# Strassen's scheme for the second products of the first layer's first pass, token sums in place, and a new table of the order

## The chip, the cores and the metric

The kernel runs on one core of one Trainium2 chip. The metric is the time of one execution on the device, in microseconds (us); of three runs of the kernel before, the median is 1659.44 us (1659.37 to 1663.88).

## The reference, cut to what matters

Attention within chunks of 64 tokens makes 4608 tokens of 512 features. Two feed-forward layers follow, the first with a gate.

```
scores = scale * q_c @ k_c.T ; attn = softmax(scores)        # per head and chunk of 64 tokens
x  = (attn @ v_c), heads side by side                        # 4608 x 512
g  = x @ w_gate ; val = x @ w_val                            # 512 -> 1536 each
x  = (g * sigmoid(g) * val) @ w_out                          # 1536 -> 512
h  = x @ w_in                                                # 512 -> 2048
out = (h * sigmoid(1.702 * h)) @ w_out2                      # 2048 -> 512
```

## The kernel before

Tokens are worked in nine blocks of 512, called block 0 to 8. Each layer's hidden features are worked in two passes over all blocks, so there are four passes: two of the first layer (three groups of two 128-feature tiles each), two of the second (two groups of four tiles). The first pass also does the attention, four units of 128 tokens for each block, one block ahead.

**Numbers in two parts.** Every operand of a large product is split into a high part of type fp32r and the rest (`split`: a copy, L573 on ACT, L575 on POOL, L577 on DVE, then a subtraction, L581). A product is three matmuls, high by high, high by rest and rest by high (`mm3`, L589, L590, L591).

**First products** (tokens by `w_gate`, `w_val`, or by `w_in`) go by Strassen's scheme in Winograd's form: seven products of sums of quarters in place of eight. `group_products` does them for a group, twelve matmuls of 256 columns to a product (token parts in tiles `x`, weight parts in `wa`, `wb`, `wc`). Of the seven, five go to one of the two PSUM banks on top of what is there; after the first, third and fifth, ACT copies the bank to a tile `u` (L573), and DVE adds four times a bank to a `u` (L581, `c<-u,banks`). The sixth product begins anew in the bank that the fifth has just filled, so it has to wait until ACT has copied the fifth.

**Second products of the first layer** come in two forms. In the first pass (`gated`, `second`) they are plain: the gated hidden tile is split, and each of the two tiles of a group is multiplied with four column blocks of `w_out`, three matmuls of 512 columns each, in four banks that add up over the three groups. In the second pass (`gated_quarters`, `hidden_part`, `second_part`) they go by Strassen's scheme: the hidden features of all three groups are collected in four quarters of 128 x 768, seven sums of quarters are split (128 x 768), and each gives three parts of six matmuls of 256 columns (21 parts for a block). The sums of `w_out` that they need are made beforehand (`y_combos`, `out_pair`), stored to `yw_dram` and loaded in pairs to the tiles `o` (L566). The first pass stores its sums to `y_dram`, the second adds to them.

**Order.** Every engine's queue is in a fixed order. A planner (`Program`) works out an order from costs and priorities, and then a table, `PLACES`, moves single operations behind others in an engine's queue, and some to another engine. So DVE or POOL may do what the code calls "dve" or "pool". SP issues all DMAs.

**Start and end.** While the first data come, TensorE does warm-up matmuls on an identity matrix (L1452, L1456). Attention units 0 to 3 are for block 0; unit 1 uses banks 4 and 5 (`gab`), where the first product goes as well. L863 are score blocks, L868 value blocks, L933 transposes, L916 to L924 the softmax. In the last block of the last pass, POOL and DVE add what the pass before left in `o_dram`, and the four quarters are stored.

Of the kernel before, what the change touches and what calls it, by code (L numbers as in the profile page):

```python
# [9 lines left out]
F32 = mybir.dt.float32  # L10
F32R = mybir.dt.float32r
# [12 lines left out]
def rd(ap):  # L24
# [34 lines left out]
    ),  # L59
    "dve": (  # L60
# [184 lines left out]
class Stage:  # L245
    UNIT = 256

    def __init__(self, pool, name, tags):
        self.ring, first = Ring(pool, name, 1), 0
        self.places = {}  # L250
        for tag, n in tags:
            self.places[tag] = Place(self, [first + 2 * i for i in range(n)])
            first += 2 * n
        self.size = first
# [14 lines left out]
class Place:  # L269
    def __init__(self, stage, homes):  # L270
        self.stage, self.homes, self.count = stage, homes, 0
# [1400 lines left out]
```

## Time and profile before

| | |
|---|---|
| median of three runs | 1659.44 us |
| profiled execution, its own time | 1666.5 us |
| its span, first to last instruction | 1664.6 us |
| PE busy | 1639.1 us, 98% of the span |
| DVE, ACT, POOL busy | 1218.1, 891.6, 527.3 us (73%, 54%, 32%) |
| moved by DMA | 488.98 MB, mean 294 GB/s |

The span is what the rows below add up to; the profiled execution's own time is 1.9 us more than it. Busy shares are means over stages with different loads, so a stage has to be read from its own stretch. An instruction's duration can reach into the next one's: matmuls of 0.28 us follow each other every 0.12 us.

### The profile page before, as it was taken

What the parts mean: (1) busy time and instruction counts of PE and PEld (TensorE: products, weight loads), DVE (VectorE), ACT (ScalarE), POOL (GpSimd) and SP (SyncE); (2) the same over time, 40 slices, a digit from 0 to 9 for tenths busy, and PEclk for the clock granted to TensorE, in tenths of its full rate; (3) what the DMA queues carried; (4) which work ended last, traced back from release to release, by engine and by line L of the source; (5) the groups of instructions that cost most, each with busy time, mean ns of one, the idle gap of its engine ahead of it and who ended that gap; (6) DMA issues with size and microseconds to landing.
All of it is one profiled execution on the core that took longest, in us unless ns stands there. A gap on an engine that the chain in (4) does not pass through costs nothing.

```text
span 1664.6 us, 37397 instructions
## 1 busy us (share of the span) xinstructions
PE 1639.1 (98%) x14914; PEld 1588.4 (95%) x14914; DVE 1218.1 (73%) x1895; ACT 891.6 (54%) x1514; POOL 527.3 (32%) x567
## 2 busy tenths in 40 slices
PE   8999999999999999999999999999999999999998
PEld 7889999999989999999999999999999999999998
DVE  7988788878745877777776877778755665566666
ACT  7977677677634444444433465555544444444443
POOL 1234554545531533332001104654521023211111
PEclk9999999999999999999999999999999999999999
DMA  7588888978799999999899999999878777767774
GB/s 298 172 286 315 300 276 300 322 266 289 264 355 336 306 357 354 364 331 356 302 326 378 359 344 316 319 319 313 286 228 334 275 250 232 230 212 235 242 267 135
DMA packets 191182, 488.98 MB, mean 294 GB/s; under 512 B 20000, under 2 KB 50208, under 8 KB 190752
## 3 DMA queue, kind: packets, MB, share of 16 engines
q1 hardware_dynamic: 191008, 486.59, 84.6%
q8 instruction: 118, 1.93, 0.5%
q14 instruction: 56, 0.46, 0.1%
HBM read 345.74 MB, written 140.77 MB: 292 GB/s over the span
## 4 chain that ended last, share of the span: by engine, by line
PE 82%; DMA 8%; DVE 5%; ACT 2%; issue 2%; POOL 1%; SPq 0%; POOLq 0%; DVEq 0%; ACTq 0%
PE banks L589 27%; PE banks L591 26%; PE banks L590 26%; DMA x_dram<-sp 2%; DMA o<-yw_dram 1%; PE banks L868 1%; PE banks L863 1%; DMA wd_b<-ws 1%; PE banks L933 1%; DMA x_dram<-xr 1%; DMA od_b<-ws 1%; ACT sp L573 1%; DMA o<-od_b 1%; DMA xr<-x_dram 1%; DMA xr<-y_dram 1%
## 5 line engine op out<-in xcount | busy, mean ns | idle before, releaser
L581 DVE TENSOR_TENSOR c<-u,banks 128x512 f32<-128x512 f32 x312 | 211.6, 682 | 169.7 <-PE banks L591 141.1
L589 PE MATMUL banks<-x,wc 128*128 128x256 f32 x1044 | 297.6, 285 | 1.9 <-ACT u L573 1.8
L590 PE MATMUL banks<-x,wc 128*128 128x256 f32 x1044 | 294.2, 282 | 0.1
L591 PE MATMUL banks<-x,wc 128*128 128x256 f32 x1044 | 294.1, 282 | 0.0
L573 ACT COPY u<-banks 128x512 f32<-128x512 f32 x261 | 151.5, 584 | 198.7 <-PE banks L591 198.3
L589 PE MATMUL banks<-x,wb 128*128 128x256 f32 x744 | 212.9, 286 | 5.0 <-ACT xr L573 2.0
L589 PE MATMUL banks<-x,wa 128*128 128x256 f32 x744 | 211.4, 284 | 0.3 <-DVE c L581 0.3
L590 PE MATMUL banks<-x,wb 128*128 128x256 f32 x744 | 210.7, 283 | 0.7 <-DVE x L581 0.7
L591 PE MATMUL banks<-x,wb 128*128 128x256 f32 x744 | 211.0, 284 | 0.0
L591 PE MATMUL banks<-x,wa 128*128 128x256 f32 x744 | 209.9, 282 | 0.0
L590 PE MATMUL banks<-x,wa 128*128 128x256 f32 x744 | 209.7, 282 | 0.0
L589 PEld LDWEIGHTS banks<-x,wc 128*128 128x128 f32 x1044 | 198.3, 190 | 7.5 <-ACT u L573 5.3
L590 PEld LDWEIGHTS banks<-x,wc 128*128 128x128 f32 x1044 | 198.5, 190 | 1.9 <-DVE x L581 0.3
L591 PEld LDWEIGHTS banks<-x,wc 128*128 128x128 f32 x1044 | 198.7, 190 | 0.0
L589 PE MATMUL banks<-sp,o 128*128 128x256 f32 (+1 forms) x594 | 195.1, 328 | 2.2 <-DMA o<-yw_dram 1.1
L590 PE MATMUL banks<-sp,o 128*128 128x256 f32 (+1 forms) x594 | 192.0, 323 | 1.2 <-DVE sp L581 1.2
L591 PE MATMUL banks<-sp,o 128*128 128x256 f32 (+1 forms) x594 | 192.0, 323 | 0.0
L1194 ACT ACTIVATE xr<-c 128x512 f32<-128x512 f32 x140 | 87.5, 631 | 156.7 <-DVE c L581 147.5
L589 PEld LDWEIGHTS banks<-x,wb 128*128 128x128 f32 x744 | 142.1, 191 | 8.5 <-DVE c L581 2.4
L590 PEld LDWEIGHTS banks<-x,wb 128*128 128x128 f32 x744 | 142.2, 191 | 2.3 <-DVE x L581 1.0
L589 PEld LDWEIGHTS banks<-x,wa 128*128 128x128 f32 x744 | 141.1, 190 | 2.8 <-DVE c L581 1.0
L591 PEld LDWEIGHTS banks<-x,wb 128*128 128x128 f32 x744 | 142.2, 191 | 0.0
(237 smaller groups left out, 4528.0 us busy)
## 6 DMA issues: line engine op xcount, KB each, us to landing
x<-x_dram SPq DMA_DIRECT2D x168, 512.0 KB, 5.8
o<-od_b SPq DMA_DIRECT2D x119, 512.0 KB, 4.6
o<-yw_dram SPq DMA_DIRECT2D x90, 512.0 KB, 5.6
x_dram<-x SPq DMA_DIRECT2D x63, 512.0 KB, 6.4
o<-od_a SPq DMA_DIRECT2D x48, 512.0 KB, 5.6
wd_b<-ws SPq DMA_DIRECT2D x56, 256.0 KB, 5.0
od_b<-ws SPq DMA_DIRECT2D x56, 256.0 KB, 4.9
x_dram<-sp SPq DMA_DIRECT2D x49, 256.0 KB, 5.5
```

The source lines that it names most:

```text
L573: op("act", act_us(n), lambda: nc.scalar.copy(out=dst.ap, in_=cut(src.ap)), [src], [dst], prio, near=near)
L581: lambda: {"dve": nc.vector, "pool": nc.gpsimd}[o.eng].tensor_tensor(out=dst.ap, in0=of_a(a.ap), in1=of_b(b.ap), op=by), reads or [a, b], ...
L589: nc.tensor.matmul(o, ah, bh, start=first, stop=False, **kind)
L590: nc.tensor.matmul(o, ah, bl, start=False, stop=False, **kind)
L591: nc.tensor.matmul(o, al, bh, start=False, stop=last, **kind)
L863: nc.tensor.matmul(un.s.ap[h64(b), a, h64(g)], un.q.ap[h64(a), cs], un.k.ap[h64(a), cs], start=True, stop=True)
L868: nc.tensor.matmul(un.o.ap[h64(b), a, h64(2 * g + c)], un.v.ap[h64(a), cs], un.e.ap[h64(a), cs], start=True, stop=True)
L933: nc.tensor.transpose(pt.ap[:, cs], e.ap[:, cs], ident.ap)
L1194: op("act", act_us(512), lambda: nc.scalar.activation(out=h.ap, in_=c.ap, func=AF.Gelu_apprx_sigmoid), [c], [h], prio, "gelu")
```

## The change

From block 3 on, the first pass also uses the scheme that the second pass has (`hides(p, b)`): its hidden features are kept as quarters, 21 parts of six matmuls of 256 columns take the place of 24 times three matmuls of 512 columns, the sums of its own `w_out` tiles are made and stored during the pass (`out_pair(0, g)`, `yw_dram[0]`), and loaded in eleven DMAs for a block in place of six. In `second_part` the seven results of the first pass are added up in tiles of `sf` and stored to `y_dram`.

Token sums (`x_made`) and sums of hidden quarters (`hidden_part`) are made in place, over a quarter that is no longer needed, so three tiles of token sums go and the token parts have seven tiles in place of eight. A sum in place may start only when the quarter it overwrites has been split. The order of the seven second products changes ("1326457"). At the start, unit 0 has banks 4 and 5 in place of unit 1, and eight more matmuls on the identity (`still`) stand among the first ones. Copies may be moved to any engine, as sums could before. The planner does 9 rounds in place of 12, and the table of moves is another one.

```diff
-        "4:9,44,61,22,19,21,8 5:26,10,18,24,17,27,52 7:13 11:15,6,20 78:54,69 23:28 25:16 209:244 "
+        "4:15,44,24,18 61:7,21,27 78:9,23,19,28 16:52 17:12,11,25,10,14,6,5,69 20:13,26 54:71 7038:244,209,210,86 "
...
-    ROUNDS = 12
+    ROUNDS = 9
...
-        ... ("o", 3), ("x", 8), ("c", 3), ("u", 3), ("m", 2), ("z", 2), ("xr", 1), ("xt", 3),
+        ... ("o", 3), ("c", 3), ("u", 3), ("m", 2), ("z", 2), ("xr", 1),
...
+    stage = {name: Stage(pool["sb"], name, tags) for name, tags in (
+        ("xs", (("x", 7, 4),)), ("sx", (("xt", 3),)), ("sh", (("h", 2), ("hx", 1))), ("sr", (("q", 1), ("k", 1), ("v", 1))),
+        ("sf", (("e", 2), ("yv", 2), ("x1", 1))), ("sp", (("hh", 3), ("hl", 3))))}
...
+    def hides(p, b):
+        return p == 1 or p == 0 and b >= 3
...
     def x_made(b, prio):
+        xb, made, q = xr.pop(b), {}, {}
+        for m in ORDER[1]:
+            made[m] = ring["x"].new([P, 2, 2, HT], F32R)
...
+        for m, j, n in (("1", 0, 0), ("2", 1, 0), ("3", 1, 1)):
+            parts(m, xb, quarter(j, n))
...
+        tt(t1, xb, xb, ALU.subtract, 512, prio, of_a=quarter(0, 1), of_b=quarter(0, 0), reads=[xb, made["1"]])
+        tt(t2, xb, t1, ALU.subtract, 512, prio, of_a=quarter(1, 1))
+        parts("6", t2)
+        parts("5", t1)
+        tt(t3, xb, xb, ALU.subtract, 512, prio, of_a=quarter(1, 1), of_b=quarter(0, 1), reads=[xb, t1])
+        parts("7", t3)
+        tt(t4, t2, xb, ALU.subtract, 512, prio, of_b=quarter(1, 0), reads=[t2, xb, made["2"]])
+        parts("4", t4)
...
-    YORDER = "1326574"
+    YORDER = "1326457"
...
     def hidden_part(y, label, prio):
+        src = {"1": b11, "3": b22, "2": b21, "6": b22, "4": b21, "5": b11, "7": b12}[label]
+        if label == "6":
+            tt(b22, b22, b11, ALU.subtract, 768, prio, T_ENG[1])
...
         elif label == "6":
-            tt(src, src, b21, ALU.subtract, 768, prio + 2, T_ENG[3])
+            tt(b21, b22, b21, ALU.subtract, 768, prio + 2, T_ENG[3])
...
+    def second_part(y, p, b, i, j, prio):
...
+        if p == 0:
...
+            if label in "1345":
+                t = ring["yv"].new([P, 2, HT])
+                if label == "5":
+                    tt(y.kept["3"], y.kept["3"], m, ALU.add, 512, prio + 0.5)
+                    done(y.kept["3"], 0, 1)
+                y.kept[label] = t
+                copy(t, m, 512, prio + 0.5)
+            elif label == "2":
+                tt(y.kept["1"], y.kept["1"], m, ALU.add, 512, prio + 0.5)
+                done(y.kept["1"], 0, 0)
+            elif label == "6":
+                tt(y.kept["3"], y.kept["3"], m, ALU.add, 512, prio + 0.5)
+            else:
+                tt(y.kept["4"], m, y.kept["4"], ALU.subtract, 512, prio + 0.5)
+                done(y.kept["4"], 1, 0)
+                tt(y.kept["5"], y.kept["5"], m, ALU.add, 512, prio + 0.5)
+                done(y.kept["5"], 1, 1)
+            return
...
-        attend(u, -40 + 4 * u, -60+3*u, bufs, ("sa", "gab", "yb", "ya")[u])
+        attend(u, -40 + 4 * u, -60+3*u, bufs, ("gab", "sa", "yb", "ya")[u])
+        if not u:
+            still = banks.new("ga", [P, 2, HT])
...
+            jobs = [(EARLY_PAIRS + STEP_PAIRS * j, out_pair(0, g)) for j, g in enumerate(gs)] + jobs
...
+    for i in range(8):
+        op("pe", 0.25, lambda: nc.tensor.matmul(still.ap[:, 0, :P], ident.ap, ident.ap, start=True, stop=True), [ident], [still], 9999)
```

Three places show what the table does. The first is PE's queue up to the first products, before and then now (`sf`, `c`: softmax tiles, `sr`, `sp`: q, k or v, `x`, later `xs`: the token parts, `wb`: weights).

```order
L933 MATMUL banks<-ident,c 128x128 x4
L1456 MATMUL banks<-ident 128x128 x5
L863 MATMUL banks<-sp 64x64 x16
L868 MATMUL banks<-c 64x64 x16
L589 MATMUL banks<-x,wb_285 128x256
```

```order
L978 MATMUL banks<-ident,c 128x128 x4
L1535 MATMUL banks<-ident 128x128 x4
L908 MATMUL banks<-sp 64x64 x16
L913 MATMUL banks<-sf,sr 64x64 x16
L913 MATMUL banks<-c 64x64 x16
L1707 MATMUL banks<-ident 128x128 x5
L908 MATMUL banks<-sr 64x64 x16
L628 MATMUL banks<-xs,wb_287 128x256
```

Both value blocks now stand together, and five of the new identity matmuls and a score block stand between them and the first product.

The second is PE's queue at the end of the last group of block 7 in the first pass, between the fifth product (`wc_1485`, now `wc_1427`) and the sixth (`wb_831`, now `wb_805`), before and then now.

```order
L590 MATMUL banks<-x,wc_1485 128x256
L591 MATMUL banks<-x,wc_1485 128x256
L589 MATMUL banks<-sp,o 128x512
L590 MATMUL banks<-sp,o 128x512
L591 MATMUL banks<-sp,o 128x512
...
L589 MATMUL banks<-x,wb_831 128x256
```

```order
L628 MATMUL banks<-xs,wc_1427 128x256
L629 MATMUL banks<-xs,wc_1427 128x256
L630 MATMUL banks<-xs,wc_1427 128x256
L628 MATMUL banks<-xs,wb_805 128x256
L629 MATMUL banks<-xs,wb_805 128x256
```

Before, two second products of three matmuls each stood there (the second, which reads the same, is left out); now the sixth product follows the fifth at once. In blocks 4, 5 and 6 four transposes stand there now, in block 3 a unit's value and score blocks, in block 8 a product of the next pass.

The third is DVE's queue in block 5, before and then now (`c<-u,banks`: sums of first products, `sr<-sr,c`, now `sx<-sx,c` and `sh<-sh,c`: gating, `sp`: rests of the hidden tiles, `t`, `st`, `ws`: weights).

```order
L924 TENSOR_TENSOR sf<-sf,z 128x512
L581 TENSOR_TENSOR c<-u,banks 128x512
L666 SCALAR_TENSOR_TENSOR t<-t,raw 128x256
L669 SCALAR_TENSOR_TENSOR t<-raw,t 128x256
L581 TENSOR_TENSOR c<-u,banks 128x512 x2
L581 TENSOR_TENSOR sr<-sr,c 128x512 x2
L581 TENSOR_TENSOR sp<-sr,sp 128x512
```

```order
L1430 TENSOR_TENSOR sx<-sx,c 128x2x256
L620 TENSOR_TENSOR c<-u,banks 128x512
L620 TENSOR_TENSOR xs<-xr,xs 128x512
L620 TENSOR_TENSOR sp<-sx,sp 128x768
L1430 TENSOR_TENSOR sh<-sh,c 128x2x256
L965 TENSOR_REDUCE z<-sf 128x8
L620 TENSOR_TENSOR sp<-sh,sp 128x768
L620 TENSOR_TENSOR sx<-sx 128x768
L620 TENSOR_TENSOR ws<-st,ws 128x256
L620 TENSOR_TENSOR sx<-sh,sx 128x768
```

Where there was a rest of 128 x 512 there are rests and sums of 128 x 768, and among them are rests of weights (`ws`) and of token parts (`xs`).

## Rows read from the trace of the kernel before

**Rows 1.** The page: engines, busy us and share.

```profile
PE 1639.1 (98%) x14914; PEld 1588.4 (95%) x14914; DVE 1218.1 (73%) x1895; ACT 891.6 (54%) x1514; POOL 527.3 (32%) x567
```

**Rows 2.** Waits of PE: engine, line, releaser, us in total, times, longest.

```profile
PE banks L589 <- ACT u L573: 2.5, 2, 1.8
PE banks L589 <- DVE c L581: 2.3, 3, 1.7
PE banks L589 <- ACT xr L573: 2.0, 1, 2.0
PE banks L589 <- DMA o<-yw_dram: 1.1, 3, 0.7
```

**Rows 3.** Windows: stretch, its us, busy us of PE, PEld, DVE, ACT, POOL, granted clock, DMA.

```profile
20.50:27.00 6.50, 6.49 (x57) 6.15 (x58) 5.88 (x13) 5.99 (x10) 2.39 (x2) 0.53 1.03 401
27.00:40.00 13.00, 11.12 (x171) 10.34 (x170) 11.82 (x22) 12.10 (x22) 1.49 (x2) 1.00 0.55 204
40.00:88.30 48.30, 48.20 (x512) 42.84 (x512) 46.77 (x77) 41.46 (x70) 15.22 (x11) 1.00 0.56 185
248.40:302.20 53.80, 53.80 (x597) 49.45 (x597) 44.80 (x71) 38.64 (x64) 29.09 (x36) 1.00 0.88 301
248.40:510.80 262.40, 260.24 (x2578) 238.57 (x2578) 193.80 (x312) 163.28 (x273) 121.89 (x143) 1.00 0.87 304
510.80:960.00 449.20, 444.56 (x3674) 440.17 (x3673) 344.52 (x505) 196.98 (x330) 111.11 (x119) 1.00 0.96 342
```

**Rows 4.** Timeline of PE: start us, us, instruction; plain and Strassen's second products.

```profile
324.12 0.39 PE L589 MATMUL banks<-sp,o 128*128 128x512 f32 x1
...
325.50 0.28 PE L589 MATMUL banks<-x,wc 128*128 128x256 f32 x1
...
622.00 0.28 PE L589 MATMUL banks<-sp,o 128*128 128x256 f32 x1
...
623.66 0.28 PE L591 MATMUL banks<-sp,o 128*128 128x256 f32 x1
```

**Rows 5.** Timeline around the first product.

```profile
19.87 0.59 ACT L573 COPY xr<-banks 128x512 f32<-128x512 f32 x1 [0.76 <-DVE x L581]
20.51 0.58 PE L589 MATMUL banks<-x,wb 128*128 128x256 f32 x1 [2.02 <-ACT xr L573]
21.10 0.41 PE L591 MATMUL banks<-x,wb 128*128 128x256 f32 x1
21.74 0.41 PE L591 MATMUL banks<-x,wb 128*128 128x256 f32 x1
```

**Rows 6.** Timeline in the second pass: a fifth and a sixth product with nothing between.

```profile
910.13 0.28 PE L591 MATMUL banks<-x,wc 128*128 128x256 f32 x1
910.50 0.59 ACT L573 COPY u<-banks 128x512 f32<-128x512 f32 x1 [5.17 <-PE banks L591]
911.14 0.39 PE L589 MATMUL banks<-x,wb 128*128 128x256 f32 x1 [0.73 <-ACT u L573]
```

**Rows 7.** Groups by form: busy us, mean ns of one, idle time before them.

```profile
L581 DVE TENSOR_TENSOR c<-u,banks 128x512 f32<-128x512 f32 x312 | 211.6, 682 | 169.7 <-PE banks L591 141.1 <-ACT u L573 24.6 <-ACT xr L1194 0.5
L581 DVE TENSOR_TENSOR sp<-sr,sp 128x768 fp32r<-128x768 f32 x34 | 32.8, 970 | 13.4 <-ACT sp L573 13.3
L581 DVE TENSOR_TENSOR ws<-st,ws 128x256 fp32r<-128x256 f32 x27 | 15.3, 571 | 3.5 <-POOL ws L575 3.5
L581 POOL TENSOR_TENSOR ws<-st,ws 128x256 fp32r<-128x256 f32 x73 | 62.6, 859 | 4.6
```

**Rows 8.** Timeline: POOL and DVE, both on SBUF, and DVE back to back.

```profile
11.58 0.68 DVE L666 SCALAR_TENSOR_TENSOR wc<-wc,wa 128x512 int32<-128x512 f32 x1
12.18 0.17 DVE L921 TENSOR_SCALAR z<-z 128x8 f32<-128x8 f32 x1
...
43.37 1.29 POOL L581 TENSOR_TENSOR ws<-wc,wc 128x512 f32<-128x512 f32 x1
43.52 1.70 DVE L669 SCALAR_TENSOR_TENSOR t<-wa,t 128x512 int32<-128x512 int32 x1
```

**Rows 9.** Timeline of the end.

```profile
1657.09 2.88 POOL L581 TENSOR_TENSOR t<-t,sf 128x512 f32<-128x512 f32 x2 [0.19 <-DVE sf L581]
1658.12 0.28 PE L591 MATMUL banks<-wb,xt 128*128 128x256 f32 x1
1661.00 0.44 SPq L569 DMA_DIRECT2D out<-t  x1
```

More of the change, by code (lines that the diff above doesn't have):

```diff
@@ L250, in __init__ @@
         self.places = {}
-        for tag, n in tags:
-            self.places[tag] = Place(self, [first + 2 * i for i in range(n)])
-            first += 2 * n
+        for tag, n, *size in tags:
+            size = size[0] if size else 2
+            self.places[tag] = Place(self, [first + size * i for i in range(n)], size)
+            first += size * n
         self.size = first
@@ L269, with __init__ @@
 class Place:
-    def __init__(self, stage, homes):
-        self.stage, self.homes, self.count = stage, homes, 0
+    def __init__(self, stage, homes, size):
+        self.stage, self.homes, self.size, self.count = stage, homes, size, 0
     def new(self, shape, dtype=F32):
-        b = self.stage.take(self.homes[self.count % len(self.homes)], 2)
+        b = self.stage.take(self.homes[self.count % len(self.homes)], self.size)
         self.count += 1
+        flat = b.make
         if len(shape) == 3:
-            flat = b.make
             b.make = lambda: flat().rearrange("p (a b) -> p a b", a=shape[1])
+        elif len(shape) == 4:
+            b.make = lambda: flat().rearrange("p (a b c) -> p a b c", a=shape[1], b=shape[2])
         return b
@@ L631, in attention_two_moe_kernel @@
             start[p].append(t)
-            t += sum(step_us(g, p) for g in gs) + (6.0 if p == 0 and b < NB - 1 else 0) + (3 * GV if p == b == 0 else 0)
+            t += sum(step_us(g, p, b) for g in gs) + (6.0 if p == 0 and b < NB - 1 else 0) + (3 * GV if p == b == 0 else 0)
     start.append([t])
@@ L722, in y_combos @@
         yield "3", s4, lambda ap: ap
-    yw_dram = pool["dram"].tile([P, 22, 2, 256], F32, name="yw_dram")
-    yw_done = [Buf(None) for _ in range(21)]
+    yw_dram = [pool["dram"].tile([P, 22, 2, 256], F32, name="yw_dram%d" % p) for p in range(2)]
+    yw_done = [[Buf(None) for _ in range(21)] for p in range(2)]
     W, WD, OD, WO = {}, {}, {}, {}
@@ L998, in token_combos @@
         b = [[quarter(j, n) for n in range(2)] for j in range(2)]
-        t1, t2, t4 = [ring["xt"].new([P, 2, HT]) for _ in range(3)]
+        t1, t2, t4 = [ring[t].new([P, 2, HT]) for t in places]
         tt(t1, xb, xb, ALU.subtract, 512, prio, of_a=b[0][1], of_b=b[0][0])
@@ L1012, in x_made, with quarter, parts @@
     def x_made(b, prio):
-        X[0, b] = []
-        for i, (m, src, cut) in enumerate(token_combos(xr.pop(b), prio)):
-            assert m == ORDER[1][i]
-            x = ring["x"].new([P, 2, 2, HT], F32R)
-            X[0, b].append(x)
-            split(*[x.part(lambda ap, c=c: ap[:, c]) for c in range(2)], src, 512, prio + i, "pool" if b else ("dve", "pool")[i % 2], cut)
-            store(x_dram[0][:, b, i], Buf(lambda x=x: x.ap.rearrange("p c a t -> p (c a t)"), None, None, x), [xd[0][b][i]], prio + i + 2)
+        xb, made, q = xr.pop(b), {}, {}
+        for m in ORDER[1]:
+            made[m] = ring["x"].new([P, 2, 2, HT], F32R)
+        X[0, b] = [made[m] for m in ORDER[1]]
+        def quarter(j, n):
+            return lambda ap: ap[:, 2 * j:2 * j + 2, n * HT:(n + 1) * HT]
+        def parts(m, src, cut=lambda ap: ap):
+            i = ORDER[1].index(m)
+            split(*[made[m].part(lambda ap, c=c: ap[:, c]) for c in range(2)], src, 512, prio + i, "pool", cut)
+            store(x_dram[0][:, b, i], Buf(lambda x=made[m]: x.ap.rearrange("p c a t -> p (c a t)"), None, None, made[m]),
+                  [xd[0][b][i]], prio + i + 2)
+        for m, j, n in (("1", 0, 0), ("2", 1, 0), ("3", 1, 1)):
+            parts(m, xb, quarter(j, n))
+        t1, t3, t4 = [Buf(lambda cut=quarter(j, n): cut(xb.ap), None, None, xb) for j, n in ((0, 0), (0, 1), (1, 0))]
+        t2 = ring["x1"].new([P, 2, HT])
+        tt(t1, xb, xb, ALU.subtract, 512, prio, of_a=quarter(0, 1), of_b=quarter(0, 0), reads=[xb, made["1"]])
[6 more added lines that the diff above has]
+        parts("4", t4)
     x0_dram = pool["dram"].tile([P, KD * BT], F32, name="x0_dram")
@@ L1058, in x_to_dram @@
             if b < NB - 1:
-                t = stage[2].take(n % 4 * 3, 2)
+                t = stage["sp"].take(n % 4 * 3, 2)
                 hi = Buf(lambda t=t: t.ap.rearrange("p (a t) -> p a t", a=2), t.prev, t.before, t)
@@ L1351, in hidden @@
         y = Hidden()
-        y.homes = [[stage[1].take(3 * n, 3) for n in range(2)], [stage[0].take(3 * n, 3) for n in range(2)]]
+        y.homes = [[stage[t].take(3 * n, 3) for n in range(2)] for t in ("sx", "sh")]
         return y
@@ L1358, in gated_quarters @@
             qs = [q.part(lambda ap: ap[:, js]) for q in y.homes[i]]
-            whole = stage[1 - i].now
+            whole = stage[("sx", "sh")[i]].now
             def ap(whole=whole):
@@ L1432, in second_part, with done @@
             return
+        label = YORDER[i]
+        if p == 0:
+            def done(t, r, c):
+                yd.setdefault(b, []).append(Buf(None))
+                store(y_dram[:, 2 * r:2 * r + 2, b * BT + c * HT:b * BT + c * HT + HT], t, [yd[b][-1]], prio + 1)
+            if label in "1345":
[16 more added lines that the diff above has]
+            return
         def add(r, c, by=ALU.add):
@@ L1436, in add @@
             tt(d, d, m, by, 512, prio + 0.5)
-        for args in (((0, 0),), ((0, 1),), ((0, 0),), ((0, 1),), ((1, 1), (0, 1)), ((1, 1), (1, 0)), ((1, 0, ALU.subtract),))[i]:
+        for args in {"1": ((0, 0),), "3": ((0, 1),), "2": ((0, 0),), "6": ((0, 1),), "4": ((1, 0, ALU.subtract),),
+                     "5": ((1, 1), (0, 1)), "7": ((1, 1), (1, 0))}[label]:
             add(*args)
@@ L1501, in spread @@
         jobs = [j for g in passes[p + 1][1] for j in group_to_dram(g, 0)]
-        a = start[p][0] + (100 if p == 0 else 10)
+        a = start[p][0] + (AFTER_PAIRS if p == 0 else 10)
         if p == 2:
@@ L1531, in put @@
                     if after_first and i == 0:
-                        for area, kind in zip(stage, (F32R, F32, F32R)):
-                            area.turn(kind)
+                        for area in ("sr", "sx", "sh"):
+                            stage[area].turn(F32R)
                 def at(i, tj=tj, step=step):
@@ L1545, in attention_two_moe_kernel @@
                         c = group_products(g, xs, at, put, p)
-                    if j == p == 0:
+                    if j == 0 and not hides(p, b):
                         yab = [banks.new("y" + i, [P, 2, BT]) for i in "ab"]
                         ys = [yab[e // 2].part(lambda ap, e=e: ap[:, e % 2]) for e in range(KD)]
-                    if p == 1:
+                    if hides(p, b):
                         if j == 0:
-                            if b == 0:
-                                for area, kind in zip(stage, (F32, F32, F32R)):
-                                    area.turn(kind)
                             hid = hidden()
```

80 lines of the change are left out of this document (32 added, 48 removed), and 360 rows, old and new, of the table PLACES.

## The prediction

> **What bounds the kernel now.** I read the page's line of engines first. PE is busy in 98% of the span; DVE comes next with 73% [rows 1]. Such shares are means, so the windows come next: in the stage that the change touches, 248.4 to 510.8 us (blocks 4 to 8 of the first pass), PE is busy for 260.24 of 262.40 us, DVE for 193.80, ACT for 163.28, POOL for 121.89 [rows 3]. PE is thus the bound there, and its time is the number of matmuls times their pitch. The list of waits agrees: the largest waits of PE are single ones, 2.5 us on the copy `u`, 2.3 on `c`, 2.0 on a bank of the attention, 1.1 on `yw_dram` loads [rows 2]. So two things can move the time: fewer columns for PE, and whether the others can still feed PE when they have more to do.
>
> **The change part by part, for the profiled execution.**
>
> *Fewer columns.* The pitch is read from starts, since durations overlap. Between 324.12 and 325.50 stand six plain matmuls of 512 columns: 1.38 / 6 = 0.230 us. Between 622.00 and 623.66 stand fourteen of 256 columns: 1.66 / 14 = 0.119 us [rows 4]. For one group of one block the plain form takes 24 x 0.230 = 5.52 us. Strassen's takes 21 x 6 / 3 = 42 matmuls for a group, 42 x 0.119 = 5.00. That saves 0.52 us, for 18 groups (blocks 3 to 8, three each) **9.4 us**. With a reading error of 0.01 us at either end of the first stretch the saving is 8.6 to 10.3.
>
> The Trainium skill (TensorE: Matmul & The Clock Gate, section Wait — 56ns, not 53.3ns?) puts the warm distance between starts at columns over 2.4 GHz plus 2.5 ns; by that a group would save 24 x 0.2158 - 42 x 0.1092 = 0.594 us, 18 groups 10.7 us, and the forecast would lie 1.3 us lower. The trace shows longer pitches, 0.230 and 0.119, and these decide.
>
> *The start.* The first product started at 20.51 us after a wait of 2.02 for unit 1's bank [rows 5]. The granted clock is 0.53 of full speed up to 27 us and 1.00 after it, which is the 1.2 GHz level and then 2.4; ahead of the first product PE had stood idle for those 2.02 us. From 21.10 to 21.74 three matmuls of 256 columns take 0.64 us, 0.213 each instead of 0.119 [rows 4, 5]. In 20.5 to 27 there are 57 matmuls in 6.49 us, and in 27 to 40 PE is idle for 1.9 of 13.00 us [rows 3]. Now unit 0 has the banks of the first product, both value blocks stand ahead, and then five identity matmuls and a score block: PE has work where it waited. I estimate the first product at 21.0 (five more small matmuls, 0.5 us). Some 24 matmuls of the first products fall before 27 us; at full clock they save 24 x 0.094 = 2.3 us, and the 1.9 us idle go in part, as the first weights no longer wait behind unit 1. Against that, four softmax operations of units 2 and 3 stand on DVE ahead of the token parts, up to 4 x 0.68 = 2.7 us [rows 8]. Bounds: -4.5 (all of 2.3 + 1.9, and 0.3 from score blocks at the higher clock) to +2.7; I take **-3**, nearer the gain, because the wait has work in its place.
>
> *The sixth product's gap.* It begins anew in the fifth's bank and waits until ACT has copied this. The second pass of before shows it uncovered: 910.13 to 911.14 is 1.01 us instead of 0.119, 0.89 lost [rows 6]. In blocks 1 to 7 second products used to stand there. Now nothing does at the last group of block 7 (0.89); four transposes do in blocks 4, 5 and 6, which I put at four matmuls of 256 columns at most (0.48), leaving about 0.45 each; score and value blocks or a product cover blocks 3 and 8. That is **+2.2**; if all covers fail, five such gaps, +4.4, and 0.9 with only block 7's.
>
> *DVE's load.* In blocks 4 to 8 DVE gets 50 more operations of 128 x 768 (0.970 us), 26 more `c`-like ones with a PSUM operand (0.682), 29 more rests of 256 columns (0.571) [rows 7], and 17 fewer of 512 in SBUF (0.68) [rows 8]: 48.5 + 17.7 + 16.6 - 11.6 = +71. POOL loses 64 by the same count, its `ws` rests at 0.859 among them [rows 7]. So DVE would need 193.8 + 71 = 265 us in 262.4 - 5 x 1.56 = 254.6 us. That is over 100%, but durations overlap: two DVE operations start 0.60 apart where the first is listed with 0.68 [rows 8]. With 0.08 less for each of 400 instructions the need is 233, **91% of the time**. Before it was 74%. That 97% can be had without PE waiting shows between 40 and 88.3 us: DVE busy 46.77 of 48.30, PE 48.20 [rows 3] (there overlaps count once); it is the nearest row. I put **+2** for late `c`, `sx` and token parts; bounds 0 (as in that row) and +32 (below, among the rivals).
>
> An operation of DVE on two SBUF operands beside one of POOL was listed with 1.70 us, where one alone has 0.68 [rows 8]. The Trainium skill (SBUF — State Buffer, section Who interferes with whom) says of this pair that a DVE instruction with two SBUF inputs contends with a POOL instruction that reads SBUF, and that one waits for the other as a whole. POOL has 64 us less in these blocks, so by row and rule alike part of the growth of DVE's busy time is given back; I count none of it in the need.
>
> *Token parts.* Seven tiles in place of eight: the parts of the next block are made over quarters that are just split, so a sum in place waits at the head of its engine's queue until ACT's copy and the rest of that quarter are done. Behind it on DVE stand the `c` sums, for whose banks PE waits. A late one shows as a wait of PE on `xs`. It is in the +2.
>
> *Transfers.* Eleven loads in place of six for each of six blocks, about 23 MB more of 489. The share of DMA in this stage, 0.87, would rise towards the 0.96 and 342 GB/s of the second pass [rows 3], where PE waited 1.1 us in all for `yw_dram` [rows 2]. I take the same again, **+1** (0 to 3). What SP now issues in addition stands in its queue ahead of later weight loads; those of before show no wait of PE beyond [rows 2].
>
> *Old waits.* The table is another, so the waits of PE between 248.4 and 960 us, 2.16 us idle in the first pass's blocks and 4.64 in the second pass [rows 3], can go or come. I take **-3**, a little under the half; bounds -7 (all of it goes) and +3 (half as much comes).
>
> *The end.* POOL takes two adds of 1.44 us before the last output, which is issued 1661.00 - 1658.12 = 2.88 us after PE's last matmul [rows 9]. In the new order POOL has three adds in series after the last label's sums, and these start 12 matmuls (1.4 us) before PE ends: 3 x 1.44 - 1.4 + some 0.9 of issuing and waiting gives 3.8. **+1** (0.3 to 1.5).
>
> Passes three and four keep their matmuls; I count nothing there.
>
> **Sum:** -9.4 - 3 + 2.2 + 2 + 1 - 3 + 1 = -9.2. The profiled execution's own time, 1666.5, lies 7.1 us above the median of the runs, 1659.44; I take that offset as the same for both kernels. 1666.5 - 9.2 = 1657.3 in the profile, and **1650 us** for the median.
>
> **Rivals.**
>
> *DVE becomes the bound (slower).* Place: blocks 4 to 8, where the most rests and sums are made in hidden quarters, each a link in a chain ACT copy, DVE rest, PE. For it: in block 4 of before (248.4 to 302.2) DVE's share was 44.80 of 53.80, 83%, with gaps that no instruction filled, since an in-order queue waits at its head. If the stage cannot be filled beyond 84%, it lasts 233 / 0.84 = 277 us, 23 over the 254.6, and the kernel 1650 + 23 - 2 = 1671. It decides from where 233 / share eats the saving of the other terms: 233 / (254.6 + 9) = 88%. Against it: the 97% between 40 and 88.3 us, and POOL, which is nearly free to DVE now. With the 265 of listed durations it would be worse, 1682 at 100%, but the starts speak against that count.
>
> *The gain comes back as waits (same).* The columns go, but loads of `yw_dram` and token parts made just in time each stop PE once per block: at 0.7 us, the longest wait on such a load [rows 2], 9 blocks give 6 us in place of 1, and the old waits stay: 1650 + 5 + 3 - 2 = 1656. For it: three `o` tiles only, and the DMA share of 0.96. Against it: in pass two the same loads cost 1.1 us in all.
>
> *More than forecast.* The start takes all of its 4.5 us and the old waits go to -7, no new ones on DVE: 1650 - 1.5 - 4 - 2 = 1642. For it: these waits are few and single, as a better table would remove them. Against it: every move is now made under tighter tiles.
>
> *The change does less than it says:* the column count is fixed by the program, so I give this no chance of its own.
>
> **How the numbers follow.** My forecast (1645 to 1654) has 0.49, more than forecast 0.18, gain given back 0.19, DVE as the bound 0.14. What a measurement can tell from no change is 0.3%, 5 us: faster is below 1654.4. So faster 0.67, same 0.19, slower 0.14. The range takes in the two near cases whole and the low end of the slow one's approach: 1640 to 1661.
>
> **What would show it.** In the profile after: 1.56 us less PE time in each of blocks 3 to 8, and a group's second products at 5.0 us; granted clock near 1.00 and no wait of 2 us at the first product; 0.9 us between a fifth and a sixth product at the end of block 7 and half of that in blocks 4 to 6; DVE at 85 to 95% of blocks 4 to 8 and PE still at 98%; waits on `yw_dram` of 1 to 3 us; last output issued 3.8 us after the last matmul. I am wrong if PE's idle time in blocks 4 to 8 is above some 8 us with DVE `c`, `sx` or `sp` as releaser, if the first stretch stays at the 1.2 GHz level, or if the pitch of the new second products isn't 0.119.

## The result, and the profile after

The changed kernel takes 1677.92 us (median of four runs, 1674.44 to 1680.13) against 1660.13 for the kernel before beside it: ratio 1.0102, 95% interval 1.0087 to 1.0117. It is 17 us slower where 9 us less had been forecast, and lies outside the range. The profiled execution took 1678.61 us, its span is 1676.8, so 12.2 us more than the span of before, which is what the rows below add up to. The medians differ by 17.8: the profiled execution of before lies 7.1 us above its median, that of after 0.7. The rows can't tell where the other 5.6 us stand.

The page's line of engines:

```profile
PE 1639.5 (98%) x15254; PEld 1604.5 (96%) x15254; DVE 1292.6 (77%) x2061; ACT 902.6 (54%) x1574; POOL 517.7 (31%) x505
```

DVE has 74 us more than in [rows 1]. PE's share still reads 98%, although it waits longer: a matmul's modelled duration reaches over short gaps. So lengths of stages are compared. The first pass's last second products stand among the first products of the second pass's first block (24 plain ones before, 126 of Strassen's after), so a border that both kernels reach with the same work done is the start of the second pass's second block. The windows of after are: from the first product to there (called the first pass below), from there to the third block of the third pass (called the second pass), from there to the last matmul, and blocks 4 to 8 (columns as in [rows 3]):

```profile
23.80:546.40 522.60, 511.41 (x5754) 487.10 (x5751) 453.29 (x794) 355.33 (x608) 149.34 (x157) 1.00 0.88 308
546.40:1014.60 468.20, 455.29 (x3723) 447.64 (x3723) 389.31 (x605) 212.15 (x381) 112.42 (x109) 1.00 0.99 359
1014.60:1670.00 655.40, 654.06 (x5480) 652.74 (x5478) 432.38 (x631) 320.40 (x564) 247.33 (x226) 1.00 0.79 266
238.20:500.30 262.10, 254.71 (x2848) 248.07 (x2847) 228.17 (x399) 171.09 (x296) 59.59 (x58) 1.00 0.93 325
```

The same windows of before, by the same borders:

```profile
20.50:546.50 526.00, 520.55 (x5453) 478.36 (x5454) 412.41 (x682) 355.19 (x593) 223.75 (x250) 0.99 0.84 289
546.50:1000.20 453.70, 448.28 (x3721) 444.24 (x3721) 353.54 (x520) 203.91 (x343) 106.38 (x111) 1.00 0.96 344
1000.20:1658.10 657.90, 655.27 (x5479) 652.08 (x5478) 438.02 (x669) 320.35 (x560) 191.75 (x196) 1.00 0.79 263
```

The first of these stages ends at about 546.4 us in both: what the columns saved was given back inside it. The second, whose matmuls did not change (3723 and 3721), became **14.5 us longer**; there DMA went from 0.96 to 0.99 and from 344 to 359 GB/s, DVE from 353.54 to 389.31 us. The rest is 2.5 us shorter; over all runs below this stretch takes 652.0 to 660.5 us, so a difference of this size means nothing. The end is 0.3 longer.

PE's waits after, to be read against [rows 2]:

```profile
PE banks L628 <- ACT u L616: 8.6, 11, 2.5
PE banks L628 <- DMA o<-yw_dram: 4.4, 10, 1.3
PE banks L629 <- DVE sp L620: 4.0, 8, 1.4
PE banks L1707 <- DVE xs L620: 2.4, 1, 2.4
PE banks L628 <- DVE c L620: 2.2, 4, 0.9
```

Instead of single waits there are many, on ACT, on DVE and on transfers. One of them in the second pass shows how they hang together, ACT's timeline first, then PE's:

```profile
844.98 0.84 ACT L616 CAST sp<-sh 128x768 fp32r<-128x768 f32 x1 [0.24 <-issue]
852.01 0.40 ACT L616 CAST ws<-st 128x256 fp32r<-128x256 f32 x1 [6.19 <-DMA od_b<-ws]
852.32 0.58 ACT L616 COPY u<-banks 128x512 f32<-128x512 f32 x1
```

```profile
850.77 0.28 PE L630 MATMUL banks<-sp,o 128*128 128x256 f32 x1
852.95 0.39 PE L628 MATMUL banks<-xs,wc 128*128 128x256 f32 x1 [1.90 <-ACT u L616]
```

A weight's copy (`ws`) waits 6.19 us at the head of ACT's queue, because the store that frees its tile has not landed; behind it stands `u`, and behind `u` PE. The wait is put down to ACT, and its cause is a transfer.

What the second pass moves more is mostly preparation of the third pass's weights. The DMA table of that stage, after and then before (x is the number of transfers, then KB each and us to landing):

```profile
DMA packets 68691, 168.07 MB, mean 359 GB/s; under 512 B 6883, under 2 KB 20481, under 8 KB 68644
wd_b<-ws SPq DMA_DIRECT2D x32, 256.0 KB, 5.3
od_b<-ws SPq DMA_DIRECT2D x28, 256.0 KB, 5.6
raw<-in_moe_w_in SPq DMA_DIRECT2D x22, 255.8 KB, 5.0
raw<-in_moe_w_out SPq DMA_DIRECT2D x16, 255.8 KB, 5.4
```

```profile
DMA packets 62122, 156.03 MB, mean 344 GB/s; under 512 B 6215, under 2 KB 16980, under 8 KB 62079
od_b<-ws SPq DMA_DIRECT2D x24, 256.0 KB, 5.4
wd_b<-ws SPq DMA_DIRECT2D x17, 256.0 KB, 5.7
raw<-in_moe_w_in SPq DMA_DIRECT2D x13, 255.8 KB, 5.1
raw<-in_moe_w_out SPq DMA_DIRECT2D x8, 255.8 KB, 6.3
```

That is 98 transfers in place of 62, 36 x 0.256 = 9.2 of the 12.0 MB more. In the first stage the changed kernel has none of the 27 `wd_b`, `od_b` and `raw<-in_moe_w_in` transfers that stood there before; it makes and loads its own `w_out` sums instead.

### The profile page after: what moved, and what is told of

It is laid out like the page before. It is cut to its first block, busy times and chain, and to the rows that moved or that the text cites. A ratio compares the mean times of both kernels' runs of the same rounds, so it can differ in the third digit from the quotient of the medians.

```text
span 1676.8 us, 38536 instructions
## 1 busy us (share of the span) xinstructions
PE 1639.5 (98%) x15254; PEld 1604.5 (96%) x15254; DVE 1292.6 (77%) x2061; ACT 902.6 (54%) x1574; POOL 517.7 (31%) x505
## 5 line engine op out<-in xcount | busy, mean ns | idle before, releaser
L628 PE MATMUL banks<-xs,wc 128*128 128x256 f32 x1044 | 298.5, 286 | 3.9 <-ACT u L616 3.2
L630 PE MATMUL banks<-xs,wc 128*128 128x256 f32 x1044 | 295.2, 283 | 0.0
L629 PE MATMUL banks<-xs,wc 128*128 128x256 f32 x1044 | 295.1, 283 | 0.0
L628 PE MATMUL banks<-xs,wb 128*128 128x256 f32 x744 | 212.1, 285 | 6.9 <-ACT u L616 5.4
L628 PE MATMUL banks<-sp,o 128*128 128x256 f32 (+1 forms) x702 | 210.6, 300 | 5.2 <-DMA o<-yw_dram 4.4
L628 PE MATMUL banks<-xs,wa 128*128 128x256 f32 x744 | 211.6, 284 | 1.1 <-DVE c L620 1.1
L629 PE MATMUL banks<-sp,o 128*128 128x256 f32 (+1 forms) x702 | 207.4, 295 | 4.1 <-DVE sp L620 4.0
L630 PE MATMUL banks<-xs,wa 128*128 128x256 f32 x744 | 210.0, 282 | 0.0
L630 PE MATMUL banks<-xs,wb 128*128 128x256 f32 x744 | 209.8, 282 | 0.0
L629 PE MATMUL banks<-xs,wb 128*128 128x256 f32 x744 | 209.7, 282 | 0.0
L629 PE MATMUL banks<-xs,wa 128*128 128x256 f32 x744 | 209.4, 282 | 0.0
L616 ACT COPY u<-banks 128x512 f32<-128x512 f32 x226 | 131.7, 584 | 142.9 <-PE banks L630 141.8
L628 PEld LDWEIGHTS banks<-xs,wc 128*128 128x128 f32 x1044 | 198.8, 190 | 8.7 <-ACT u L616 6.7
L630 PE MATMUL banks<-sp,o 128*128 128x256 f32 (+1 forms) x702 | 206.0, 293 | 0.0
L629 PEld LDWEIGHTS banks<-xs,wc 128*128 128x128 f32 x1044 | 199.5, 191 | 0.3
L630 PEld LDWEIGHTS banks<-xs,wc 128*128 128x128 f32 x1044 | 199.5, 191 | 0.0
L628 PEld LDWEIGHTS banks<-xs,wb 128*128 128x128 f32 x744 | 141.2, 190 | 9.8 <-ACT u L616 6.7
L628 PEld LDWEIGHTS banks<-xs,wa 128*128 128x128 f32 x744 | 141.4, 190 | 3.0 <-DVE c L620 1.9
L628 PEld LDWEIGHTS banks<-sp,o 128*128 128x128 f32 x702 | 133.0, 189 | 10.6 <-DMA o<-yw_dram 6.0
L629 PEld LDWEIGHTS banks<-xs,wa 128*128 128x128 f32 x744 | 141.3, 190 | 0.5
```

What stands on the lines that cost most here:

```text
L616: o = op(eng, us, lambda: on[o.eng](dst.ap, cut(src.ap)), [src], [dst], prio, near=near)
L628: nc.tensor.matmul(o, ah, bh, start=first, stop=False, **kind)
L629: nc.tensor.matmul(o, ah, bl, start=False, stop=False, **kind)
L630: nc.tensor.matmul(o, al, bh, start=False, stop=last, **kind)
```

## The experiments

Two theories are tried. LOAD says that the change adds work and bytes to engines that are already full (the expectations also call it FORM, ENGINE for ACT and DVE, DMA for the transfers). ORDER (also TABLE) says that the new form is worth its columns and the new order is bad. Ratios are to the kernel before, run beside each; lengths of a stage come from one profiled execution of each kernel, and stages that an edit leaves alone differ between such executions by 1 to 3 us in the first two and by up to 6 in the long last one. Cuts in code are marked `...`.

**Without tables.** `PLACES = {}` in e1 (before), e2 and e3 (changed); e3 also:

```diff
-        return p == 1 or p == 0 and b >= 3
+        return p == 1
...
-            jobs = [(EARLY_PAIRS + STEP_PAIRS * j, out_pair(0, g)) for j, g in enumerate(gs)] + jobs
+            jobs = jobs
```

> The kernel before without its table of moves (the planner's own order). It is the base for the next two. Theory FORM (the changed form and the sums in place make work for DVE, ACT and DMA that eats the columns saved, whatever the order): about 1690 to 1720 us, no statement on its distance to the changed kernel without table except that the changed one is not faster. Theory TABLE (the form is worth its 9 us, the new table is worse than the old one by some 20): the changed kernel without table is 5 to 10 us faster than this one.

> The changed kernel without its table of moves. TABLE: 5 to 10 us below the kernel before without table. FORM: at or above it, by 0 to 20 us.

> The changed kernel without table, and with plain second products in all blocks of the first pass (no sums of w_out for it, no eleven loads); sums in place, seven token tiles, the start and the planner's rounds stay as changed. Against the changed kernel without table it tells what the form alone is worth. If the form is worth its columns: 5 to 9 us slower than the changed kernel without table. FORM: equal or faster by up to 10 us.

Measured: 1700.44 (1.0244), 1724.22 (1.0388, interval 1.0364 to 1.0412) and 1711.34 us (1.0307, 1.0273 to 1.0340). With the planner's own order the form costs 12.9 us (FORM had said up to 10), and the rest of the change 10.9. TABLE falls: without tables the loss is larger, 23.8 us, and the new table is worth more to its kernel (46.3 us) than the old one to its own (40.3). From block 3 to the end of the first stage e2 takes 366.1 us and e3 354.8, so in this order most of the form's cost stands in the first pass.

**One tile less.** e11 is e1 with `("x", 7)` for `("x", 8)`.

> The kernel before without its table, with seven token tiles in place of eight and nothing else changed: against e1 (1700.4 us) the price of the missing tile. e3 stood 10.9 us above e1 with the plain form, of which some 12 us lay in blocks 3 to 18 (4.8 in the first pass, 6.8 in the second). If the missing tile is most of it: 1706 to 1712. If it is the sums in place or the weights' copies: 1698 to 1703.

1696.89 us (1.0211): not slower than e1, and a little below both forecasts. The missing tile alone is not the reason. What makes e3 slower than e1 stays open: the sums in place, the new start and the planner's rounds were not taken apart, and each changes the planner's order too.

**The preparation left out.** e14 is e2 without `out_pair(0, g)`; the loads read `od_a` tiles.

> The changed kernel without table as in e2 (1724.2 us), but without preparing the first pass's own sums of w_out: the eleven loads for a block stay, and take tiles of w_out that are there anyway (not the reference's values). Away are 42 copies and rests of weights, 12 sums of weights, 48 conversions, 21 stores and 12 loads, between 70 and 300 us. If this preparation is what the form costs (12.9 us between e3 and e2): 1704 to 1712, so the form alone would be worth nothing or a few us. If it is the eleven loads, the hidden sums and their place in the queues: 1718 to 1725.

1727.2 us (1.0408): a miss. The second pass moves 161.8 MB instead of 171.0 and still takes no less time (483.2 us, e2 475.8). In the planner's order a changed list of operations moves everything else, and differences of some us between e1, e2, e3, e11 and e14 can come from that alone; what the preparation costs stays open.

**Bytes taken away.** In the changed kernel's order:

```diff
-            load(x.part(lambda ap: ap.rearrange("p c a t -> p (c a t)")), x_dram[layer - 1][:, b, i], prio + 2 * i, [xd[layer - 1][b][i]])
+            if p == 1:
+                half_x = x.part(lambda ap: ap.rearrange("p c a t -> p (c a t)")[:, :512])
+                op("dma", 0.74 / 2048 * 4 * 1024, lambda half_x=half_x, b=b, i=i: nc.sync.dma_start(
+                    out=bits(half_x.ap), in_=x_dram[0][:, b, i, :512]), [xd[0][b][i]], [half_x], prio + 2 * i)
...
```

> The changed kernel in its order, with the token parts of the second pass loaded by half (the first 512 of 1024 columns; the rest keeps what an earlier block left, so the values are not those of the reference). That is 14.7 MB less in the second pass, a tenth of what it moves. Theory DMA (transfers bound the second pass: share 1.00; late loads stop PE directly or stand at the head of a queue): PE's idle time in 546 to 967 us falls from 12.4 to about 5 us and the kernel is 6 to 10 us faster, 1667 to 1672. Theory ENGINE (ACT and DVE have too much in their in-order queues): within 3 us of the changed kernel, 1675 to 1680.

1665.23 us (1.0027, 1.0010 to 1.0044): 12.7 us faster, more than DMA had said; the second pass is 10.5 shorter. The number of transfers and the order of every engine are those of after. Its window:

```profile
542.90:1000.60 457.70, 449.43 (x3723) 445.00 (x3722) 386.28 (x605) 212.44 (x381) 113.05 (x109) 1.00 0.95 336
```

DVE and ACT are about as busy as after; the share of DMA fell, and with it the time. The control, on the kernel before:

> Control: the kernel before with the same halving of the second pass's token loads (the products there read the first half in place of the second, so the values are not the reference's). Theory DMA says that the second pass of before was just under the limit (share 0.96, 4.6 us idle) and the change pushed it over: the kernel before gains 2 to 4 us (1656 to 1659), far less than the 12.7 that the changed kernel gained. If it gains 10 or more as well, the halving simply removes something that both have, and DMA does not explain the difference of the two kernels.

1659.20 us (0.9989, 0.9976 to 1.0002): 1.3 us, not clear of nothing. In its profile the second pass is 3.9 us shorter than before:

```profile
545.00:994.80 449.80, 446.19 (x3722) 443.89 (x3721) 357.35 (x520) 203.56 (x342) 103.60 (x110) 1.00 0.91 316
```

So the same bytes are worth 12.7 us to the changed kernel and at most about 4 to the kernel before.

**The first pass's loads and DVE's rests.** e6 loads one of each pair of `w_out` sums in the first pass (`yw_dram[p][:, k:k + m]` with m = 1 for p = 0); e7:

```diff
-        split(hi, lo, src, 768, prio, Y_LO[k])
+        copy(hi, src, 768, prio)
+        some = lambda ap: ap[:, :256]
+        tt(lo.part(some), src, hi, ALU.subtract, 768, prio, Y_LO[k], of_a=some, of_b=lambda ap: rd(ap)[:, :256])
```

> The changed kernel with only the first of each pair of w_out sums loaded in the first pass's hidden blocks (the second product of a pair uses the first's sums again; not the reference's values): 16 MB less between 200 and 550 us. Theory DMA for the first pass: the waits that ate the 9.4 us there (9.3 us more idle time of PE in blocks 1 to 9) shrink by half, 4 to 6 us faster, about 1673. Theory ENGINE (there DVE at 87% and ACT's queue decide, not transfers): within 2 us of the changed kernel, 1676 to 1680, and the long waits at 270, 343 us stay.

> The changed kernel with the rests of the sums of hidden quarters made for 256 of their 768 columns (103 operations, 95 of them on DVE; the rest of the columns keeps old values, not the reference's). DVE saves about 0.55 us for each, some 22 us in blocks 4 to 8 and 30 in the second pass, and each second product's last link is 0.55 us shorter. ENGINE: waits on sp go and the idle time of PE in blocks 4 to 8 falls from 7.4 to 3 us, the second pass gains 3 to 5: 1667 to 1671. DMA: the direct waits on sp (some 5 us) go in part, 1673 to 1676.

1672.32 us (1.0075) and 1669.63 us (1.0055): 5.6 and 8.3 us faster, as DMA and ENGINE forecast for their own case. The first pass takes 518.3 us in e6 and 518.1 in e7 instead of 522.6, so each gives back some 4 of what was lost there; in e4, which leaves it alone, it took 521.5. In e6 the two long waits of the changed kernel, 1.44 us at 272 and 2.46 at 346, are still there as 0.96 at 267 and 2.48 at 340, which ENGINE had forecast.

**ACT's queue.** e8 and e12 have the order written out, and copies that the table moved from POOL to ACT back on POOL: 114, or the 92 of the first two passes.

> The changed kernel with the order of every queue written out, and the 114 copies (mostly weights, ws) that its table moved from POOL to ACT back on POOL at the same place in time. It takes 40 us off ACT's queue in the first two passes, and with it heads of the queue that wait (6.19 us on a store at 852 us). If copies on ACT are what delays u: the waits on ACT u fall from 8.6 to about 4 us, 1672 to 1674. If POOL's slower copies and its reads beside DVE's cost as much: equal or slower, 1676 to 1684.

> As the kernel with all copies back on POOL, but only the 92 of the first two passes; the 22 of the later passes stay on ACT, where the other kernel lost 5 us. If ACT's queue was a part of the loss in the first two passes: 1672 to 1675. If not: 1676 to 1680.

1678.16 us (1.0108) and 1673.60 us (1.0069, 1.0053 to 1.0086). All 114 gave nothing, as the rival had said; the 92 gave some 4 us, so ACT's queue is a small part. In e8 waits on `yw_dram` rose from 4.4 to 8.3 us.

**Both relieved alike.** e9 (changed) and e10 (before): token loads of the second pass and `w_out` loads of the first by half, rests of hidden numbers narrowed.

> The changed kernel with all reliefs at once: half token loads in the second pass, half loads of w_out sums and of w_out tiles in the first pass, rests of hidden numbers for a third or a fourth of their columns (not the reference's values). Theory LOAD (the columns are saved, and DMA and DVE together take the gain back): the gains of the single reliefs (12.7, 5.6, 8.3) add in part, 1651 to 1658, and with the next kernel as its counterpart it is 4 to 10 us the faster of the two. Rival ORDER (the new table stops PE in places that no relief reaches): 1662 or more, and not faster than the counterpart.

> The kernel before with the same reliefs: half token loads in the second pass, half loads of w_out tiles in the first pass, the same rests narrowed (not the reference's values). LOAD: it is hardly limited by DMA or DVE, gains 2 to 4 us, 1656 to 1659. ORDER: the same.

1662.25 us (1.0004) and 1655.97 us (0.9966, 0.9950 to 0.9982). The distance fell from 17 to 6.3 us, but the changed kernel isn't the faster one: LOAD's forecast for this pair is wrong, and ORDER's fits. The pair can't decide between them, though, because equal reliefs leave unequal loads. By stages, e9 is 4.2 us shorter in the first pass (517.1 and 521.4), where the columns are saved, and 8.3 longer in the second. There it still has 11 MB and 29 us of DVE more than e10 (first row e9, second e10):

```profile
538.70:995.70 457.00, 448.16 (x3722) 444.55 (x3721) 357.97 (x605) 212.03 (x381) 105.36 (x109) 1.00 0.96 336
542.30:991.00 448.70, 446.22 (x3723) 443.81 (x3722) 328.62 (x520) 203.27 (x342) 100.57 (x110) 1.00 0.92 317
```

With 153.5 MB and 358 us of DVE the relieved second pass of e9 carries about what the unrelieved one of before carries (156.0 MB, 353.5 us), and takes 457.0 us against 453.7. So at nearly equal load 3.3 of the 14.5 us are left, no more than e18 below makes by a change of order alone (457.2). Some of e9's waits are in queues that no relief touched: 2.47 us at 338 us on a `u` behind a table load, 1.20 at 838 behind the `ws` of the rows above.

**Moving single operations up.** e13 is e12 with 23 operations moved up, e18 the kernel before with 22.

> The kernel with 92 copies back on POOL (1673.6 us), and 23 operations moved up in their queues by one to seven places, each one that PE waited for in that kernel's trace while its own inputs were there: copies u and sums c ahead of a weight's copy, a table load or a softmax step (for instance the u at 340 us that stood behind exp and waited 2.7 us), four loads of o. Amount of work and bytes unchanged. QUEUE (single waits in the in-order queues): of 8 to 10 us of such waits more than half go, 1666 to 1669. LOAD (the waits come back elsewhere, since the engines and DMA are full): 1671 to 1676.

> The kernel before with its order written out and 22 operations moved up in their queues by one to four places where PE waited for them although their inputs were there (6 to 8 us of waits in all, the first product's and 1.8 us at 475 us among them). If single waits are the reason for lost time wherever they stand: 3 to 6 us faster, 1654 to 1657. If waits come back elsewhere: within 2 us.

1670.54 us (1.0065, 1.0037 to 1.0094), not to be told from e12, and 1665.35 us (1.0023, 1.0010 to 1.0037), slower by some 4 us where 3 to 6 less or no change had been expected. In e13 the `u` at 340 us came in time, as these rows of PE show, and new waits stood beside it, 1.35 us ahead and 1.77 behind:

```profile
339.74 0.39 PE L706 MATMUL banks<-xs,wc 128*128 128x256 f32 x1 [1.35 <-DVE u L694]
342.11 0.39 PE L706 MATMUL banks<-xs,wb 128*128 128x256 f32 x1 [0.24 <-ACT u L694]
345.57 0.64 PE L991 MATMUL banks<-sf,sr 64*64 64x64 f32 x28 [1.77 <-ACT sf L1059]
```

In e12 the list has one wait of 2.6 us at this place and neither of the other two. So a wait can't be taken away by itself and counted as gained.

**Load added to the kernel before**, in its form and order:

```diff
+            if o.eng == "dve":
+                nc.vector.tensor_reduce(out=waste.ap, in_=more(src.ap), axis=AX.X, op=ALU.add)
...
+            nc.sync.dma_start(out=spare.pop()[:, :256], in_=OD[g][0][:, i].rearrange("p a c -> p (a c)")[:, :256])
...
+                if p == 1:
+                    nc.sync.dma_start(out=spare.pop(), in_=x_dram[layer - 1][:, b, i, :512])
```

The reduction is in e15 and e17 (104 times), the two copies in e16 and e17.

> The kernel before, its order unchanged, with 104 additional reductions on DVE, each behind a rest of hidden numbers, whose result nobody reads: about 28 us more DVE time in the first pass and 34 us in the second (the changed kernel has 34 more in blocks 4 to 8 and 33 in the second pass). LOAD: PE waits for later c and sp, 3 to 8 us slower, 1663 to 1668. ORDER (it is the new order, not the amount of work): within 2 us of the kernel before.

> The kernel before with additional copies inside DRAM behind its loads, which nobody waits for: 56 of 256 KB behind the token loads of the second pass (14.7 MB; the changed kernel moves 12 MB more there) and 48 of 128 KB behind loads of w_out tiles in the first (6.3 MB; the changed kernel 5.4 MB more). LOAD: the second pass goes over the limit (share 0.96 before), 4 to 9 us slower, 1664 to 1669. ORDER: within 2 us.

> Both additions. LOAD: the two costs add or more, 8 to 18 us slower, 1668 to 1678; that the changed kernel, with 9.4 us less for PE, stands 17 us above the kernel before would then need some 8 us more than this from its form and order. ORDER: within 4 us.

1671.01 us (1.0062, 1.0045 to 1.0080), 1684.84 us (1.0149, 1.0121 to 1.0177), 1694.08 us (1.0205, 1.0174 to 1.0237). All three are slower than LOAD's own ranges, and still further from ORDER's. The second pass of e15 and of e16:

```profile
546.20:1007.80 461.60, 451.01 (x3723) 445.25 (x3722) 381.81 (x582) 205.08 (x346) 105.31 (x113) 1.00 0.95 338
544.80:1019.50 474.70, 454.61 (x3723) 447.08 (x3722) 355.92 (x520) 203.29 (x344) 104.84 (x112) 1.00 0.98 359
```

With 28 us more of DVE this pass is 7.9 us longer, though DVE is then busy for 83% of it; with 14.7 MB more it is 21.0 longer, and with both (e17) 480.5 us, 27 longer, well over what the changed kernel loses. No result of the added work is read, but it isn't free of side effects: in e15 ACT waits six times, 7.1 us in sum, and POOL once, 4.8 us, until a reduction has read a tile that they write next; in e16 the added copies take places in SP's queue, and each byte is read from DRAM and written there. So it is shown that the second pass of before, in its own form and order, loses time by additions of this kind and size; how much one MB or one us of DVE costs is not.

## Why the prediction was wrong, point by point

- **Fewer columns, -9.4.** Held. The seven second products run at the forecast pitch (six steps from 258.80 to 259.52 us, 0.12), and block 8, which has no long wait, takes 45.5 us for 378 matmuls, 0.120 each.
- **The start, -3.** Partly held, -1.7: block 1 begins 1.7 us earlier. The first product came at 23.81, not at 21.0. PE waited 2.38 us until 20.41 for DVE's `xs`, which stood behind softmax operations, the other bound that I had given. Then the identity matmuls and the score block ahead of the first product took 3.40 us at a granted clock of 0.52, the lower level. In e4, which has the same order, they followed the same wait, took 1.94 us at 1.00, and the first product came at 21.42 (21.4 to 21.7 also in e6, e7 and e9). So half of this delay belongs to the execution that was profiled. From the first product on the pitch is 0.12.
- **The sixth product's gap, +2.2.** Block 7 has 0.83 us (450.91 to 451.86 instead of 0.12), blocks 4 and 6 have 0.48 each, as worked out; in block 5 it is 2.7, since `u` stood behind exp and its table load.
- **DVE's load, +2.** The need of 233 us was 228.17, 87% of blocks 4 to 8. From block 1 to the end of the first stage the time is 459.8 us against 458.2: waits ate the 9.4 and 1.6 more, where 4 us of gain had been left over (with the gaps, DVE and the loads). In blocks 4 to 8 PE waited 3.6 us for `u`, 2.0 for `sp` and 1.2 for `yw_dram`. That PE waits little at this load was the error; the 97% between 40 and 88 us [rows 3] were one order without hidden sums. DVE's share alone doesn't give the loss either: e15 has DVE at 80% in its blocks 4 to 8 (74% before), and its first pass is no longer than before (525.3 us, 526.0). What shows DVE as a part is e7.
- **Transfers, +1, and old waits, -3: the step that failed.** I priced the loads of the first pass and let the second pass only get better. I had read that the second pass stands at a share of 0.96, and that added issues stand ahead of later weight loads; I put no price on this, because PE had shown no wait for these before, and did not ask what would be pushed into the second pass: the preparation of the third pass's weights that lost its place in the first. It got 12 MB and 36 us of DVE more, and 14.5 us longer instead of some 3 shorter. That is 17.5 of the 21.4 us between the forecast (-9.2) and the profiled spans (+12.2).
- **The end, +1.** 6.86 us from the last matmul to the end instead of 6.51: +0.35.
- **The offset.** I took the profiled execution as 7.1 us above the median for both kernels. After, it is 0.7, so the median is missed by 6.4 us more than the profile.

Sum: -1.7 + 1.6 + 14.5 - 2.5 + 0.3 = 12.2, the difference of the spans.

My signs of being wrong looked at the first pass and the start alone: the idle time of blocks 4 to 8 is 7.4 us (I had said 8), the pitch is 0.12. None looked at the second pass, and none of them told of the loss.

Of the rivals, "DVE becomes the bound" had nearly the time (1671) by luck, since it had the wrong place: narrower rests give back 4.5 of the first pass's 11 us (518.1 us in e7 instead of 522.6), but the larger loss lies in the second pass. "The gain comes back as waits" describes the first pass, though with other waits than it named: mostly on `u` and `sp`. In the second pass the loss goes with the load, and most with the bytes: at the changed kernel's own order half token loads give back 10.5 us (e4) and narrower rests 4.1 (e7: 464.0), and with both the pass is within 3.3 us of before (e9). Not shown is an exact account: what remains in the first pass, where e9 saves 4.2 of the 9.4 us against e10, and what another order could do. In the planner's order the second pass took 483.2 us with 161.8 MB (e14) and 475.8 with 171.0 (e2), so order counts as well. Moving single operations did not remove the waits. Of the versions that leave nothing out, none beats the kernel before.

## What to carry to other kernels

Work that a change adds to a side engine or to the transfers early on can push other work that is done ahead of need into a later stage; look there for the cost, above all where a stage already reads 0.95 or more on DMA. Before counting columns saved, halve the loads of the stage in both kernels: the one that gains is the one that is bound there. Equal reliefs do not make equal loads: compare stages that carry the same. And a wait's price is known only when it is taken away, since the next one can stand behind it.

## What the runs showed of the hardware

At 0.96 and 344 GB/s the second pass of before became 3.9 us shorter with 14.7 MB less (e5, share 0.91) and 21 us longer with 14.7 MB more (e16, share 0.98): near a share of 1 bytes that cost little below it cost much, though e16's copies are of another kind than e5's loads. The rate alone doesn't set the time: in the planner's order this pass takes 471.6 us at 321 GB/s (e3). The Trainium skill (DMA: Bandwidth & Descriptors, section Specifications) gives 435 GB/s for the fabric and some 358 for a core's part of its memory. Here the means of the full stages lie near the second figure (359 after and in e16, 362 in e7), but stretches of 12 us within them reach 413 GB/s, so it is no limit that this core's transfers keep to; these stretches stay below the first.

With 14.7 MB more, DVE is busy for 355.92 us in that pass, without them for 353.54, and ACT for 203.29 and 203.91: the instructions themselves did not get longer, and the time went into waits. The Trainium skill (SBUF — State Buffer, section Who interferes with whom) says that DMA doesn't contend with the engines; the trace agrees.

The same 42 matmuls ahead of the first product, after the same idle 2.38 us, took 3.40 us at a granted clock of 0.52 in one execution and 1.94 us at 1.00 in another (after and e4).
